# A GEGLU feed-forward kernel: bf16 products done ahead in nine groups of sixteen matmuls in place of eighteen groups of eight

## The chip, the core and the metric

The kernel runs on one core of a Trainium2 chip. The metric is the device time of one execution in microseconds (us). TensorE (PE) multiplies, its weight loads have a row of their own in the profile (PEld), VectorE (DVE), ScalarE (ACT) and GpSimd (POOL) do element-wise work, and SyncE (SP) issues nearly all the transfers. Every engine runs its own list of instructions in order and waits for others through semaphores.

## The reference

```
B, S, D, F = 32, 32, 1024, 3584
x: (B, S, D)   w_gate, w_up: (D, F)   w_down: (F, D)   all bf16

def reference(x, w_gate, w_up, w_down):
    return (_gelu(x @ w_gate) * (x @ w_up)) @ w_down
```

The gelu is the tanh approximation. There are N = 1024 rows of x; F = 3584 is cut into 28 blocks of 128, D = 1024 into 8 slices of 128.

## The kernel before

**Seven products in place of eight.** The kernel has two stages, and in each it treats a matrix product as a product of matrices of two by two blocks, done by Strassen's scheme in Winograd's form: seven block products instead of eight. In the first stage, for each of the 28 blocks `i` of F, four weight blocks (the two halves of D of the gate weights, a11 and a12, and of the up weights, a21 and a22) meet four blocks of x (two halves of D, two halves of N: B11, B12, B21, B22). Sums of weight blocks (S1 to S4) and of x blocks (T1 to T4) are kept as float32r, a 32-bit type that TensorE multiplies; the blocks themselves are bf16. Every product is four matmuls of 128x128 weights by 128x512 (function `product`, line 111).

Two of the seven products need no sums: the first, a11 by B11, and the second, a12 by B21, both bf16. The first is copied out of PSUM by ACT (L187, tile `e1`) to serve later as a seed of other products, and then the second is added onto the same bank of PSUM; its total is the gate's pre-activation for the first half of N, and ACT takes its gelu (L193, tile `gl0`). So for one block, the first product and ACT's copy come before the second product, and the second product comes before the gelu that gives the bank back. These two products depend on weights and x alone and are done ahead of the others: variable `done` counts the blocks whose first product has been issued.

The other five are float32r. In the trace they are told by their tiles: the sixth product is `x<-T,s`, the fourth `x<-T,c`, the fifth `y<-T,s`, the seventh `x<-T,s` again, the third `y<-B,s`, and the two bf16 products are `a<-xt,gw`. The sixth, seventh and fourth follow each other onto one bank `X[i]`, which ACT seeds with the copied first product (L199); ACT copies it out after the sixth (L214, tile `e2`) and after the seventh (L227, `e3`), and DVE multiplies it after the fourth (L218). The fifth and third share a bank `Y[i]`, from which DVE makes sums (L229, L234), the second of which goes through ACT's gelu (L236).

**Order of the work.** It is written out by hand (`tc.manual_schedule`): each engine executes its instructions in the order of the program, and only waits are inserted. A lead-in (lines 255 to 262) issues first and second products of eight blocks in the order first n, first n+1, second n, second n+1. Blocks 0 and 1 then go through the other five products, with two calls of `ahead`. From line 296 a loop runs over the blocks 2 to 28. One iteration `i` issues: the sums S1 and S3 of block i+1 on POOL (L166, L167), the sixth product of `i`, the seed of i+1, the fourth product of i-1, the sums S2 (DVE, L171) and S4 (POOL, L175) of i+1, the fifth product of `i`, possibly a bf16 group, the seventh product of `i`, and the third product of i-1. An iteration without a bf16 group has 20 matmuls and is called bare below. `ahead` does the first product of block `done` and the second product of block `done - 1`, eight matmuls; it is called in every iteration but those in `ALONE`, until all 28 blocks are done. Weights are fetched on SP's queue at the end of even iterations, five gate tiles of two blocks being held (L84, L91).

**Buffers.** The PSUM pool has four banks for tag `p` (the `X`) and four for tag `q`, which the `A` of the bf16 products and the `Y` share. A pool hands out the buffer that was given back longest ago in the order of the program, and the first writer of it waits for the last reader of the tile before. `E1` tiles hold two blocks each in a ring of four; a ring buffer is free once the seeds of its two blocks have been issued and done.

The second stage (lines 328 to 485) multiplies by w_down in the same manner, its operands as prepared by the first; TensorE goes from one stage to the next without a pause.

The lines that the change and the prediction touch:

Of the kernel before, what the change touches and what calls it, by code (L numbers as in the profile page):

```python
# [12 lines left out]
def kernel(  # L13
# [31 lines left out]
    FT = F // P  # L45
# [3 lines left out]
    assert N == 2 * NB and DT % 2 == 0 and D % DB == 0 and FT % 4 == 0  # L49
    NWARM = 18  # L50
    LEAD = 8
    ALONE = (4, 7, 10, 13, 16, 19)
    KF = FT // 2
    TT = NT // 2
    JF = KF // 2
# [25 lines left out]
    def load_gate(c, queue, lo=0, hi=DT):  # L81
        if c not in WG:
            WG[c] = gw.tile([P, DT, 2 * P], bf16, name="gw", tag="gw")
        queue.dma_start(  # L84
            out=WG[c][:, lo:hi, :], in_=wg_r[:, lo:hi, 2 * c * P : (2 * c + 2) * P]
        )

    def load_up(c, lo=0, hi=4):
        if c not in WU:
            WU[c] = uw.tile([P, DT, 4 * P], bf16, name="uw", tag="uw")  # L90
        nc.sync.dma_start(  # L91
            out=WU[c][:, :, lo * P : hi * P],
            in_=wu_r[:, :, (4 * c + lo) * P : (4 * c + hi) * P],
        )
# [4 lines left out]
    def a11(i):  # L99
        return block(WG, 2, i, 0)  # L100

    def a12(i):
        return block(WG, 2, i, 1)
# [7 lines left out]
    def product(ps, lhs, rhs, first=True):  # L111
        for k in range(KH):
            nc.tensor.matmul(  # L113
                ps,
                lhsT=lhs[:, k, :],
                rhs=rhs[:, k, :],
                start=(first and k == 0),
                stop=(k == KH - 1),
                skip_group_check=True,
            )  # L120
# [4 lines left out]
    def psum_q(name):  # L125
        return psum.tile([P, NB], fp32, name=name, tag="q")

    with tc.manual_schedule():
# [35 lines left out]
        def early_sums(i, engine=nc.gpsimd):  # L164
            S1[i], S3[i] = weight_tile("s1"), weight_tile("s3")
            engine.tensor_tensor(S1[i], a21(i), a22(i), ALU.add)  # L166
            engine.tensor_tensor(S3[i], a11(i), a21(i), ALU.subtract)  # L167

        def second_sum(i):
            S2[i] = weight_tile("s2")  # L170
            nc.vector.tensor_tensor(S2[i], S1[i], a11(i), ALU.subtract)  # L171

        def late_sums(i, engine=nc.gpsimd):
            S4[i], C22[i] = weight_tile("s4"), weight_tile("c22")
            engine.tensor_tensor(S4[i], a12(i), S2[i], ALU.subtract)  # L175

        def copy_a22(i):
            nc.scalar.activation(C22[i], a22(i), ACT.Copy)
# [3 lines left out]
        def first_product(i):  # L182
            A[i] = psum_q("a")
            product(A[i], a11(i), B11)
            if i % 2 == 0:
                E1[i // 2] = ring.tile([P, 2, NB], fp32, name="e1", tag="ring")
            nc.scalar.activation(E1[i // 2][:, i % 2, :], A[i], ACT.Copy)  # L187

        def second_product(i):
            product(A[i], a12(i), B21, first=False)  # L190
            if i % 2 == 0:
                GL[i // 2] = half.tile([P, 2, NB], bf16, name="gl0", tag="half")
            nc.scalar.activation(GL[i // 2][:, i % 2, :], A[i], ACT.Gelu_apprx_tanh)  # L193
# [3 lines left out]
        def seed(i):  # L197
            X[i] = psum_p("x")
            nc.scalar.activation(X[i], E1[i // 2][:, i % 2, :], ACT.Copy)  # L199

        done = 0

        def ahead():
            nonlocal done
            if done < FT:
                first_product(done)
            if done:
                second_product(done - 1)
            done += 1

        def sixth_product(i):
            product(X[i], S2[i], T["T2"], first=False)
            E2[i] = epool.tile([P, NB], fp32, name="e2", tag="e2")
            nc.scalar.activation(E2[i], X[i], ACT.Copy)  # L214

        def fourth_product(i):
            product(X[i], C22[i], T["T4"], first=False)
            nc.vector.tensor_tensor(gT[:, i, 0:NB], GL[i // 2][:, i % 2, :], X[i], ALU.mult)  # L218

        def fifth_product(i):  # L220
            Y[i] = psum_q("y")
            product(Y[i], S1[i], T["T1"])

        def seventh_product(i):
            product(X[i], S3[i], T["T3"], first=False)
            e3 = epool.tile([P, NB], fp32, name="e3", tag="e3")
            nc.scalar.activation(e3, X[i], ACT.Copy)  # L227
            U1[i] = epool.tile([P, NB], bf16, name="u1", tag="u1")
            nc.vector.tensor_tensor(U1[i], Y[i], e3, ALU.add)  # L229

        def third_product(i):
            product(Y[i], S4[i], T["B22"], first=False)
            h1 = epool.tile([P, NB], bf16, name="h1", tag="h1", bufs=1)
            nc.vector.tensor_tensor(h1, Y[i], E2.pop(i), ALU.add)  # L234
            G1[i] = epool.tile([P, NB], bf16, name="gl1", tag="gl1")
            nc.scalar.activation(G1[i], h1, ACT.Gelu_apprx_tanh)  # L236

        def finish(i):
            nc.vector.tensor_tensor(gT[:, i, NB:N], G1.pop(i), U1.pop(i), ALU.mult)
# [23 lines left out]
        done = LEAD  # L263
# [5 lines left out]
        for k in range(KH):  # L269
            for i in range(2):  # L270
# [7 lines left out]
                )  # L278
        ahead()
        sixth_product(0)  # L280
        sixth_product(1)
        seventh_product(0)
        seventh_product(1)
# [12 lines left out]
        for i in range(2, FT + 1):  # L296
            here, prev, more = i < FT, i - 1 if i > 2 else None, i + 1 < FT
            if more:
                early_sums(i + 1)
            if here:  # L300
                sixth_product(i)
                if more:
                    seed(i + 1)
            if prev:
                fourth_product(prev)
            if more:
                second_sum(i + 1)
                late_sums(i + 1)
            if prev:
                finish(i - 2)  # L310
            if here:
                fifth_product(i)
            if here and i not in ALONE and done <= FT:
                ahead()
            if here:
                seventh_product(i)
                if more:
                    copy_a22(i + 1)
            if prev:
                third_product(prev)  # L320
            if here and i % 2 == 0:
                if i // 2 + 5 < FT // 2:
                    load_gate(i // 2 + 5, nc.sync)
                if i % 4 == 0 and i // 4 + 1 < FT // 4:
                    load_up(i // 4 + 1)
# [190 lines left out]
```

## Time and profile before

| What | Value |
|---|---|
| Three runs | 277.67, 278.09 (median), 278.29 us |
| The profiled execution's own time | 277.56 us |
| Its span, first to last instruction | 275.8 us, so 1.76 us lie around it |
| Mean granted TensorE clock | 0.999 |
| TensorE busy | 270.0 us of the span (98%) |
| ACT, DVE, POOL busy | 138.1, 189.2, 88.6 us |
| The loop of lines 296 to 326, from the first sixth product to the second stage | 33.64 to 184.58 us |

How to read the rows: a row of a timeline gives the start, the duration, the engine, the line in the kernel, the operation, the tile written and the tiles read, the shapes and, in square brackets, the idle time of that engine before it and what ended it. Rows of one kind that follow each other are merged, with their number behind an x; some matmul records are missing from a trace, so that a group of eight may read x7. Matmuls are pipelined: one that lasts 379 or 389 ns in the records is followed by the next after 216 or 227 ns. Where the text speaks of nanoseconds from one start to the next, these are single records of the same trace. A window row gives busy time and number of instructions of each engine in a stretch of time.

### The profile page before, as it was taken

How to read it: one execution, taken by the hardware profiler on the slowest of the kernel's cores; microseconds unless marked ns; L12 is line 12 of the kernel's file. 1: busy time of each engine (PE TensorE's matmuls, PEld its weight loads, DVE VectorE, ACT ScalarE, POOL GpSimd, SP SyncE). 2: the span in 40 equal slices, each digit the busy share in tenths (PEclk: the TensorE clock that was granted, in tenths of full speed). 3: DMA queues.
4: the chain of work that ended last, by engine and by line, in shares of the span. 5: the costliest groups of instructions: out<-in, count | busy, mean ns of one | idle time of the engine just before them, and what ended most of it. 6: DMA issues, size and time to landing. Idle time of an engine off the chain costs nothing.

```text
span 275.8 us, 3328 instructions
## 1 busy us (share of the span) xinstructions
PE 270.0 (98%) x1179; PEld 190.5 (69%) x1194; DVE 189.2 (69%) x227; ACT 138.1 (50%) x237; POOL 88.6 (32%) x81
## 2 busy tenths in 40 slices
PE   8999999999999999999999999999999999999995
PEld 3446767777677776777766777764447888888883
DVE  0279865667666676666766555759994999999900
ACT  2488475665656665666656666532100082870311
POOL 0000484458554585545854444600000000000000
PEclk9999999999999999999999999999999999999999
DMA  8996420522062071152420120259702000000221
GB/s 194 286 280 157 150 71 5 156 77 76 18 212 76 0 225 37 46 154 76 154 76 9 67 58 22 88 188 324 239 0 76 2 0 0 0 2 0 96 96 38
DMA packets 40912, 26.42 MB, mean 96 GB/s; under 512 B 9152, under 2 KB 40896, under 8 KB 40896
## 3 DMA queue, kind: packets, MB, share of 16 engines
q1 hardware_dynamic: 40224, 25.82, 32.0%
q10 hardware_dynamic: 672, 0.39, 0.5%
q8 instruction: 9, 0.15, 0.2%
q14 instruction: 7, 0.06, 0.1%
HBM read 22.02 MB, written 2.10 MB: 87 GB/s over the span
## 4 chain that ended last, share of the span: by engine, by line
PE 96%; DMA 3%; issue 0%; ACT 0%
PE x L113 28%; PE x L371 18%; PE y L113 18%; PE a L113 17%; PE y L371 9%; PE z L371 4%; DMA xt<-in_x_dram 3%; PE y L271 1%; ACT o_sb L483 0%
## 5 line engine op out<-in xcount | busy, mean ns | idle before, releaser
L113 PE MATMUL x<-T,s 128*128 128x512 f32 x224 | 63.5, 408 | 0.0
L113 PE MATMUL a<-xt,gw 128*128 128x512 bf16 x212 | 51.0, 380 | 1.1 <-DMA xt<-in_x_dram 0.4
L175 POOL TENSOR_TENSOR s<-gw,s 128x512 fp32r<-128x512 bf16 x26 | 30.4, 1171 | 62.4 <-PE y L113 61.7
L113 PEld LDWEIGHTS x<-T,s 128*128 128x128 f32 x224 | 41.7, 188 | 10.8 <-ACT e L214 0.4
L229 DVE TENSOR_TENSOR u<-y,e 128x512 bf16<-128x512 f32 x28 | 19.2, 690 | 34.8 <-ACT e L227 34.1
L171 DVE TENSOR_TENSOR s<-s,gw 128x512 fp32r<-128x512 f32 x28 | 40.8, 1457 | 0.0
L113 PEld LDWEIGHTS <-gw 128*128 128x128 bf16 x224 | 20.2, 98 | 27.6 <-issue 5.7
L218 DVE TENSOR_TENSOR gT<-gl,x 128x512 bf16<-128x512 bf16 x28 | 19.1, 686 | 18.4 <-PE x L113 18.4
L236 ACT ACTIVATE gl<-h 128x512 bf16<-128x512 bf16 x28 | 17.7, 631 | 27.4 <-DVE h L234 27.4
L113 PE MATMUL x<-T,c 128*128 128x512 f32 x112 | 30.2, 393 | 0.0
L113 PE MATMUL y<-B,s 128*128 128x512 f32 x112 | 30.0, 391 | 0.0
L167 POOL TENSOR_TENSOR s<-gw,uw 128x512 fp32r<-128x512 bf16 x25 | 29.2, 1168 | 0.0
L166 POOL TENSOR_TENSOR s<-uw 128x512 fp32r<-128x512 bf16 x25 | 29.1, 1164 | 0.0
L187 ACT ACTIVATE e<-a 128x512 f32<-128x512 f32 x28 | 16.7, 597 | 22.9 <-PE a L113 22.8
L113 PE MATMUL y<-T,s 128*128 128x512 f32 x104 | 27.8, 389 | 0.0
L371 PE MATMUL x<-tc,sc 128*128 128x512 f32 x112 | 25.7, 389 | 0.0
L113 PEld LDWEIGHTS y<-B,s 128*128 128x128 f32 x112 | 21.0, 188 | 4.8
L113 PEld LDWEIGHTS x<-T,c 128*128 128x128 f32 x112 | 20.9, 188 | 4.8 <-ACT e L227 0.5
L371 PEld LDWEIGHTS x<-tc,sc 128*128 128x128 f32 x112 | 21.0, 188 | 4.4
L227 ACT ACTIVATE e<-x 128x512 f32<-128x512 f32 x28 | 16.8, 599 | 14.4 <-PE x L113 14.4
L113 PEld LDWEIGHTS y<-T,s 128*128 128x128 f32 x104 | 19.5, 188 | 4.1
L371 PEld LDWEIGHTS <-gT 128*128 128x128 bf16 x112 | 10.9, 98 | 13.2 <-issue 0.3
(52 smaller groups left out, 325.0 us busy)
## 6 DMA issues: line engine op xcount, KB each, us to landing
gw<-in_w_gate_dram SPq DMA_DIRECT2D x13, 512.0 KB, 3.9
uw<-in_w_up_dram SPq DMA_DIRECT2D x6, 1024.0 KB, 6.4
v<-in_w_down_dram SPq DMA_DIRECT2D x5, 512.0 KB, 3.8
v<-in_w_down_dram SPq DMA_DIRECT2D x4, 640.0 KB, 7.9
v<-in_w_down_dram SPq DMA_DIRECT2D x8, 256.0 KB, 4.3
out_dram<-o_sb SPq DMA_DIRECT2D x15, 128.0 KB, 1.7
uw<-in_w_up_dram SPq DMA_DIRECT2D x2, 512.0 KB, 6.0
gw<-in_w_gate_dram ACTq DMA_DIRECT2D x1, 256.0 KB, 4.4
```

The source lines that it names most:

```text
L113: nc.tensor.matmul(ps, lhsT=lhs[:, k, :], rhs=rhs[:, k, :], start=(first and k == 0), stop=(k == KH - 1), skip_group_check=True,)
L166: engine.tensor_tensor(S1[i], a21(i), a22(i), ALU.add)
L167: engine.tensor_tensor(S3[i], a11(i), a21(i), ALU.subtract)
L171: nc.vector.tensor_tensor(S2[i], S1[i], a11(i), ALU.subtract)
L175: engine.tensor_tensor(S4[i], a12(i), S2[i], ALU.subtract)
L187: nc.scalar.activation(E1[i // 2][:, i % 2, :], A[i], ACT.Copy)
L218: nc.vector.tensor_tensor(gT[:, i, 0:NB], GL[i // 2][:, i % 2, :], X[i], ALU.mult)
L227: nc.scalar.activation(e3, X[i], ACT.Copy)
L229: nc.vector.tensor_tensor(U1[i], Y[i], e3, ALU.add)
L236: nc.scalar.activation(G1[i], h1, ACT.Gelu_apprx_tanh)
L271: nc.tensor.matmul(Y[i], lhsT=S1[i][:, k, :], rhs=T["T1"][:, k, :], start=(k == 0), stop=(k == KH - 1), skip_group_check=True,)
L371: nc.tensor.matmul(ps, lhsT=lhs[:, i, t * P : (t + 1) * P], rhs=rhs[:, i, :], start=(first and j == 0 and i == 0), stop=(last and j == JF ...
```

## The change

The tuple `ALONE`, iterations that did without a bf16 group, gives way to `PAIRS`, iterations that have one. A new function `pair_ahead` does the work of two calls of `ahead` at once, in another order: the second product of block `done - 1`, the first product of `done`, the first product of `done + 1`, the second product of `done`. The last iteration of `PAIRS` (26) finds all first products done and only does the second product of block 27.

```
-    ALONE = (4, 7, 10, 13, 16, 19)
+    PAIRS = (2, 5, 8, 10, 13, 16, 18, 21, 24, 26)
...
+        def pair_ahead():
+            nonlocal done
+            second_product(done - 1)
+            if done < FT:
+                first_product(done)
+                first_product(done + 1)
+                second_product(done)
+            done += 2
...
-            if here and i not in ALONE and done <= FT:
-                ahead()
+            if i in PAIRS:
+                pair_ahead()
```

Before, groups stood in iterations 2, 3, 5, 6, 8, 9, 11, 12, 14, 15, 17, 18 and 20 to 25, with a group of four matmuls in 26. After, groups of sixteen stand in 2, 5, 8, 10, 13, 16, 18, 21 and 24, with the same group of four in 26.

## The prediction

> **What bounds the kernel now.** I read the page first: engine shares, the granted clock and the chain that ended last.
>
> ```profile
> span 275.8 us, 3328 instructions
> ...
> PE 270.0 (98%) x1179; PEld 190.5 (69%) x1194; DVE 189.2 (69%) x227; ACT 138.1 (50%) x237; POOL 88.6 (32%) x81
> ...
> PEclk9999999999999999999999999999999999999999
> ...
> PE 96%; DMA 3%; issue 0%; ACT 0%
> ```
>
> TensorE is the bound, at full clock in every slice. Work that moves on ACT, DVE, POOL or a queue costs nothing unless TensorE comes to wait for it; a wait of TensorE costs its full length. Then the loop of the change (lines 296 to 325) by windows, each from the start of one fifth product to the next:
>
> ```profile
> core 0: us, PE busy (x) PEld busy (x) DVE busy (x) ACT busy (x) POOL busy (x), PEclk, DMA share, GB/s
> 57.16:63.46 6.30, 6.30 (x30) 4.46 (x28) 3.81 (x5) 3.80 (x8) 3.41 (x4) 1.00 0.00 1
> 63.46:68.00 4.54, 4.54 (x21) 3.71 (x20) 3.82 (x5) 2.59 (x6) 3.41 (x4) 1.00 0.41 115
> ```
>
> The first is an iteration with a group of eight bf16 matmuls beside its 20 float32r ones, the second a bare one of 20. Next, the stage that already does what the change will do often: in the lead-in (timeline) a first product is followed by another first product and then by the second product on the first one's bank, which must wait for ACT's copy.
>
> ```profile
> 7.96 5.99 PE L113 MATMUL a<-xt,gw 128*128 128x512 bf16 x27 [0.43 <-DMA xt<-in_x_dram]
> ...
> 9.02 0.60 ACT L187 ACTIVATE e<-a 128x512 f32<-128x512 f32 x1 [5.66 <-PE a L113]
> 9.88 0.60 ACT L187 ACTIVATE e<-a 128x512 f32<-128x512 f32 x1 [0.27 <-PE a L113]
> ...
> 10.74 0.60 ACT L193 ACTIVATE gl<-a 128x512 bf16<-128x512 f32 x1 [0.27 <-PE a L113]
> ```
>
> 27 matmuls start within 5.99 - 0.38 = 5.61 us, 216 ns each: that wait cost nothing. In the loop (timeline again):
>
> ```profile
> 68.21 0.58 ACT L214 ACTIVATE e<-x 128x512 f32<-128x512 f32 x1
> ...
> 68.91 1.90 PE L113 MATMUL a<-xt,gw 128*128 128x512 bf16 x7
> 70.05 0.60 ACT L187 ACTIVATE e<-a 128x512 f32<-128x512 f32 x1 [0.77 <-PE a L113]
> ...
> 70.46 1.27 PE L113 MATMUL x<-T,s 128*128 128x512 f32 x4
> 70.85 0.60 ACT L193 ACTIVATE gl<-a 128x512 bf16<-128x512 f32 x1 [0.21 <-PE a L113]
> ```
>
> To be seen: the copy L214 of the sixth product ends at 68.79, 0.12 before TensorE goes on at 68.91. Two more places of the timeline show what late ACT work does. First, one of the few waits of TensorE; then iteration 2, where ACT is behind:
>
> ```profile
> 25.61 0.60 ACT L214 ACTIVATE e<-x 128x512 f32<-128x512 f32 x1 [0.20 <-PE x L113]
> ...
> 26.26 0.76 PEld L113 LDWEIGHTS x<-T,s 128*128 128x128 f32 x4 [0.20 <-ACT e L214]
> ```
>
> ```profile
> 35.46 1.90 PE L113 MATMUL a<-xt,gw 128*128 128x512 bf16 x8
> ...
> 36.58 0.59 ACT L199 ACTIVATE x<-e 128x512 f32<-128x512 f32 x1
> ...
> 37.21 0.60 ACT L187 ACTIVATE e<-a 128x512 f32<-128x512 f32 x1
> ...
> 37.70 0.59 ACT L193 ACTIVATE gl<-a 128x512 bf16<-128x512 f32 x1
> ```
>
> **The change part by part.** The count of matmuls, ACT, DVE and POOL instructions and DMAs stays. Eighteen groups of eight become nine of sixteen; the last group of four (second product of block 27, iteration 26) stays in its place. No DMA moves in its queue: gate loads are issued at the same lines and wait for POOL's sums, which the pairs do not touch. Blocks 22 and 23 move most, from iterations 20 and 21 to 18; their gate tile is asked for in iteration 12, six iterations ahead, with 3.9 us to landing.
>
> *Fewer switches.* A group adds 6.300 - 4.547 = 1.753 us to an iteration (mean of the windows above in ns), while eight bf16 matmuls at 215.8 take 1.726: 27 ns per group are the price of switching from float32r to bf16 and back. Nine go: -0.24 us. Its ends: 0, and -0.35 if the 39 ns by which an iteration with a group exceeds 20 x 226.7 + 8 x 215.8 all belong to the group.
>
> *The two new ACT waits of a pair.* Inside a pair the second product of the new block waits for the copy (L187) that began four matmuls before. Also the second first product needs a bank: banks go out in the order in which they were given back (this gives all 56 bank numbers of the program before), and by that order it takes, in eight of nine pairs, the bank that the gelu (L193) of the same pair's opening second product gave back, again four matmuls before. The chain is matmul 379, start of ACT 37 later, 597 of copy or gelu: 1,013 ns from the start of the last matmul. TensorE is due 5 x 215.8 = 1,079 after it. 66 ns are left, and in the lead-in the same 66 left no loss. Cost 0 for a wait of this form.
>
> Where the copy carries a second wait (for the ring buffer that its own earlier seed frees), ACT starts 97 after the matmul instead of 37 (52.90 and 70.05 in the loop: idle 0.83 and 0.77 before it, and only 0.21 before the gelu that follows). The chain is then 1,073. TensorE's weight load starts 52 after ACT's end (26.21 to 26.26), so a loss of 1,073 + 52 - 1,079 = 46 ns. I expect it for the pairs of iterations 5, 8 and 10, whose ring buffer was freed one or two iterations before; later pairs come three or more after. 3 x 46 = +0.14 us. Ends: 0, and 18 x 46 = 0.83.
>
> *Iteration 2.* ACT's order becomes gelu of 9, copy of 10, copy of 11, gelu of 10 behind a queue that runs to 37.18. Unwaited ACT work goes out every 0.49 there: gelu at 37.07, copy of 10 at 37.56 to 38.16, TensorE free at 38.21; due is 35.46 + 0.23 + 11 x 0.216 = 38.06. +0.15 us. This spares the 41 ns that the fourth product of iteration 3 now waits for ACT's copy (38.97). Net +0.11, ends -0.04 and +0.42 (each of the two starting only 0.03 after the other's end).
>
> *Two bare iterations in a row.* New is a bare iteration behind a bare one (4, 7, 12, 15, 20, 23). Behind a bare iteration the copy L214 ends 0.12 before the fifth product's end (68.79 against 68.91; 0.11 to 0.15 at 85.94, 103.09, 120.23, 137.41; 0.19 at 51.58), behind one with a group 0.25. Today a bf16 group stands there, which does not need the copy; now the seventh product does, as float32r, whose weight load itself waits. At 26.21 the copy also ended 0.12 before the matmul was due, and the next matmul came 268 instead of 227 later: 41 lost. Five of the six: +0.21 us; iteration 4 keeps 0.19. Ends: 0 and 6 x 0.1 = 0.6. What is late next: nothing adds up, because DVE's L218 and POOL's L175 start anew from TensorE's products in every bare iteration (DVE 3.82 and POOL 3.41 of 4.54 us busy).
>
> The sum: -0.24 + 0.14 + 0.11 + 0.21 = +0.22 us. Against the profiled execution (span 275.8, 1.76 around it, 277.56 in all) that is 277.78. It lies 0.53 below the median of the three runs, 278.09; carried to the median: 278.3.
>
> **The rivals.** *Even (0.68)*: the sum above, within 0.2% (0.56 us, about what a measurement can tell from no change). Own range 277.7 (terms at their low ends, -0.39) to 278.6.
>
> *Slower by the close waits (0.20)*: every pair's two ACT waits miss. Place: the matmuls opening the second first product and the second product; price 18 x 46 instead of 3 x 46, so 278.3 + 0.69 = 279.0. It decides once the chain is over 1,027 (1,079 - 52), only 14 ns beyond what the rows show, and loses 18 ns in all for each ns more. For it: the gelu's 599 and the copy's 601 at their longest. Against it: lag 37 and 597 in every undisturbed group of the loop.
>
> *Slower by the bank (0.03)*: the bank freed last is handed out at once, so the first new product stands behind the gelu: 1,013 + 52 - 216 = 0.85 us, nine times 7.6, less 0.24: 285.5. Against it are the 56 bank numbers. The Trainium skill (Perfetto Trace Analysis, Optimizing Tensor Performance, Matmuls) speaks against the change in this sense: independent groups should rotate through different banks so that ACT's emptying of one overlaps the next group. By that rule a bank reused within a pair would cost time; by the lead-in's rows four matmuls already hide the emptying.
>
> *The clock (0.01)*: if TensorE fell to the rate of its first warm matmuls (427 ns each) in the pairs, 9 x 16 x 0.211 = 30 us, 308. The clock row shows full speed throughout, with idle spots of 0.4. The Trainium skill (TensorE: Matmul & The Clock Gate, A second HAM failure mode: psum-queue depth-cycling) reports such an oscillation where TensorE idles briefly between groups that cycle through banks; no row here shows it.
>
> *Faster (0.08)*: switches cost more than the windows show. From 33.64 to 184.58 the loop takes 150.94; 520 x 226.7 + 148 x 215.8 make 149.8. If all 1.12 beyond came from the eighteen groups, half would go and no wait be added: 277.5.
>
> **How the numbers follow.** Likeliest: 278.3. Faster 0.08, same 0.68, slower 0.20 + 0.03 + 0.01 = 0.24. The range reaches from the faster case, 277.5, to just over the close waits, 279.1; outside lie the bank, the clock and the tails of both.
>
> **What would show it.** Right: nine bf16 groups of 16 at 216 ns per start, sixteen matmuls and no idle time inside; a pair's iteration 8.03 us, bare ones 4.55 and the second of two 4.59; weight loads waiting for ACT L214 in five or six places; a short gap in the pair of iteration 2. Wrong: waits of `a` for L193 or L187 in all pairs (close waits); gaps of 0.85 before a first product (bank); a second bare iteration much over 4.6, so that DVE or POOL do fall behind; a clock digit below 9.

## The result, and the profile after

The changed kernel takes 278.88 us (median; 278.60 to 279.09), the kernel before 277.68 in the same comparison (277.62 to 278.29). The ratio is 1.0042, 95% interval 1.0032 to 1.0052: slower by 1.2 us. That lies inside the range on record (277.5 to 279.1), but it is not the likeliest case, "even" at 278.3. The kernel came out slower, and not for the reason that the forecast gave for that case.

The profiled execution has a span of 277.3 us. TensorE is still the bound and still at full clock (page of the changed kernel):

```profile
span 277.3 us, 3330 instructions
...
PE 271.0 (98%) x1180; PEld 190.8 (69%) x1194; DVE 189.2 (68%) x227; ACT 138.0 (50%) x237; POOL 88.8 (32%) x81
...
PEclk9999999999999999999999999999999999999999
```

Windows from one fifth product to the next, iterations 6, 7, 11, 12 and 13. Of two bare iterations in a row the second is the slower one (7 and 12, against 6 and 11), and the iteration with the group of sixteen, 13, is as cheap as forecast:

```profile
core 0: us, PE busy (x) PEld busy (x) DVE busy (x) ACT busy (x) POOL busy (x), PEclk, DMA share, GB/s
59.36:63.91 4.55, 4.55 (x21) 3.76 (x20) 3.82 (x5) 2.13 (x5) 3.42 (x4) 1.00 0.01 2
63.91:68.99 5.08, 4.82 (x21) 3.68 (x20) 3.80 (x5) 3.19 (x6) 3.41 (x4) 1.00 0.35 103
89.73:94.28 4.55, 4.55 (x21) 3.72 (x20) 3.81 (x5) 2.60 (x6) 3.41 (x4) 1.00 0.39 115
94.28:98.93 4.65, 4.65 (x22) 3.68 (x20) 3.82 (x5) 2.81 (x6) 3.42 (x4) 1.00 0.00 2
98.93:106.95 8.02, 7.95 (x36) 5.25 (x36) 3.82 (x5) 5.14 (x10) 3.41 (x4) 1.00 0.63 196
```

Inside that pair (timeline) ACT's gelu and its copies follow each other at the 0.27 us of idle time that the lead-in showed, and the matmuls on record start 215 to 217 ns apart:

```profile
100.06 3.40 PE L113 MATMUL a<-xt,gw 128*128 128x512 bf16 x15
100.91 0.60 ACT L193 ACTIVATE gl<-a 128x512 bf16<-128x512 f32 x1 [0.80 <-PE a L113]
...
101.78 0.60 ACT L187 ACTIVATE e<-a 128x512 f32<-128x512 f32 x1 [0.27 <-PE a L113]
102.64 0.60 ACT L187 ACTIVATE e<-a 128x512 f32<-128x512 f32 x1 [0.27 <-PE a L113]
```

Where the 1.2 us went can be read off the lengths of the iterations, single records in ns. From the fifth product of iteration 2 to the second stage, the loop takes 150.03 us before and 151.22 after; the second stage, 91.19 and 91.21, does not change.

| Place | Difference to before, us |
|---|---|
| Nine times a pair and a bare iteration, 8.0265 + 4.547, in place of 2 x 6.300 | -0.24 |
| Pairs of iterations 5, 8, 10: 8.093 in place of 8.027 | +0.20 |
| Iterations 2 and 3: 11.886 in place of 11.753, beside the switch saved there | +0.16 |
| Second bare iterations 12, 15, 20, 23: 4.647, 4.633, 4.679, 4.687 in place of 4.547 | +0.46 |
| Second bare iteration 7: 5.081 in place of 4.547 | +0.53 |
| Other iterations, up to 33 ns each, and the end of the loop | +0.08 |

Nearly half of the loss is the one iteration 7. In the second bare iteration 12 (timeline) ACT's copy L223 (L214 before the change) ends at 95.06, and the weight load of the seventh product starts at 95.17 instead of 94.96, where the matmul ahead of it starts:

```profile
93.94 0.63 ACT L245 ACTIVATE gl<-h 128x512 bf16<-128x512 bf16 x1 [1.00 <-DVE h L243]
...
94.48 0.58 ACT L223 ACTIVATE e<-x 128x512 f32<-128x512 f32 x1
...
95.17 0.77 PEld L113 LDWEIGHTS x<-T,s 128*128 128x128 f32 x4 [0.25 <-POOL s L166]
95.21 1.16 PE L113 MATMUL x<-T,s 128*128 128x512 f32 x4
```

The waits name POOL here. The weight load stands behind two waits, POOL's and ACT's, so who really held it is a question for an experiment.

### The profile page after: what moved, and what is told of

It is laid out like the page before. It is cut to its first block, busy times and chain, and to the rows that moved or that the text cites. A ratio compares the mean times of both kernels' runs of the same rounds, so it can differ in the third digit from the quotient of the medians.

```text
span 277.3 us, 3330 instructions
## 1 busy us (share of the span) xinstructions
PE 271.0 (98%) x1180; PEld 190.8 (69%) x1194; DVE 189.2 (68%) x227; ACT 138.0 (50%) x237; POOL 88.8 (32%) x81
## 4 chain that ended last, share of the span: by engine, by line
PE 94%; DMA 3%; ACT 1%; issue 1%; DVE 0%; ACTq 0%
PE x L113 27%; PE x L380 18%; PE a L113 17%; PE y L113 17%; PE y L380 9%; PE z L380 4%; DMA xt<-in_x_dram 3%; PE y L280 1%; DVE u L238 0%; DVE h L243 0%; ACT e L236 0%; ACT o_sb L492 0%; ACT e L223 0%; ACT c L178 0%; ACT gl L245 0%
## 5 line engine op out<-in xcount | busy, mean ns | idle before, releaser
L113 PE MATMUL x<-T,s 128*128 128x512 f32 x224 | 62.3, 403 | 0.3 <-ACT e L223 0.3
L113 PE MATMUL a<-xt,gw 128*128 128x512 bf16 x213 | 48.6, 379 | 1.3 <-DMA xt<-in_x_dram 0.6
L238 DVE TENSOR_TENSOR u<-y,e 128x512 bf16<-128x512 f32 x28 | 19.3, 691 | 37.1 <-ACT e L236 35.3
L113 PEld LDWEIGHTS <-gw 128*128 128x128 bf16 x224 | 20.9, 98 | 27.8 <-issue 4.1
L245 ACT ACTIVATE gl<-h 128x512 bf16<-128x512 bf16 x28 | 17.7, 631 | 28.9 <-DVE h L243 28.9
L167 POOL TENSOR_TENSOR s<-gw,uw 128x512 fp32r<-128x512 bf16 x25 | 29.3, 1173 | 0.7 <-PE x L113 0.7
L166 POOL TENSOR_TENSOR s<-uw 128x512 fp32r<-128x512 bf16 x25 | 29.1, 1165 | 0.0
L236 ACT ACTIVATE e<-x 128x512 f32<-128x512 f32 x28 | 16.8, 599 | 20.7 <-PE x L113 20.7
L193 ACT ACTIVATE gl<-a 128x512 bf16<-128x512 f32 x28 | 16.7, 596 | 10.6 <-PE a L113 10.3
```

The costliest lines, as they stand in the source:

```text
L113: nc.tensor.matmul(ps, lhsT=lhs[:, k, :], rhs=rhs[:, k, :], start=(first and k == 0), stop=(k == KH - 1), skip_group_check=True,)
```

## The experiments

Theory: TensorE waits for ACT's copy of the sixth product wherever a bare iteration follows a bare one, and that is due to where the groups stand; the order inside the pair costs little. Rivals: the pair's own waits; POOL, as the waits say; chance, for iteration 7.

### The changed kernel again, and bare iterations two in a row without pairs

> The changed kernel once more. Theory (the new order makes TensorE wait for ACT's copy L223 in a bare iteration that follows a bare one): iterations 12, 15, 20 and 23 again take 4.63 to 4.69 us in place of 4.55, the pairs of iterations 5, 8 and 10 again show one matmul 260 ns after the one before. Open: iteration 7, which took 5.08 us. If it belongs to the order it takes 5.08 again; if DVE's late sum L238 (0.4 us after everything that it needs) was chance, it takes 4.65.

It took 278.68 us, in one run. Iterations 12, 15, 20 and 23 took 4.634, 4.626, 4.627 and 4.633, the pairs of 5, 8 and 10 8.086 to 8.087, and iteration 7 5.074. DVE's sum L238 of iteration 6 again came 0.51 us after DVE's work before it, where 0.10 would do, so 0.4 us late. So the loss of iteration 7 was not chance; it belongs to the program.

```
-    ALONE = (4, 7, 10, 13, 16, 19)
+    ALONE = (6, 7, 12, 13, 18, 19)
```

> Groups of eight as before, no pairs, but the six bare iterations stand two in a row (6 and 7, 12 and 13, 18 and 19). Theory: bare iterations 7, 13 and 19 lose about 0.09 us each to ACT's copy though there is no pair, 0.3 us in all, 0.1% slower than before. Rival (the order inside the pair and its new waits cost the time): these iterations take 4.55 us like the first of each two and the time is that of before.

278.39 us, ratio 1.0025 (1.0015 to 1.0035): slower than expected, without a single pair. Windows of iterations 12 and 13:

```profile
core 0: us, PE busy (x) PEld busy (x) DVE busy (x) ACT busy (x) POOL busy (x), PEclk, DMA share, GB/s
93.78:98.35 4.57, 4.57 (x21) 3.71 (x20) 3.81 (x5) 2.62 (x6) 3.41 (x4) 1.00 0.01 2
98.35:102.98 4.63, 4.63 (x21) 3.68 (x20) 3.83 (x5) 2.76 (x6) 3.44 (x4) 1.00 0.82 255
```

Iterations 13 and 19 took 4.626, iteration 7 took 5.026, and every iteration with a group of eight 6.300 (but the third, 6.323). So bare iterations two in a row cost 0.7 us by their place alone, with groups of eight and no pair. The expected 0.3 us was too little because iteration 7 lost 0.48 here too.

### ACT's copy ahead of the gelu

In the kernels so far ACT's list has the gelu of the third product (L245) ahead of the copy of the next sixth product, and the gelu waits for DVE. The edit puts it behind; the new function `late_gelu` does the gelu of the tile that waits in `H1`:

```
         def third_product(i):
...
-            nc.scalar.activation(G1[i], h1, ACT.Gelu_apprx_tanh)
+            H1[i] = h1
...
                 sixth_product(i)
+                late_gelu()
                 if more:
                     seed(i + 1)
```

> The changed kernel with one more edit: ACT takes the gelu of the third product (L245) after the copy of the next sixth product and not ahead of it, so that this copy ends about 0.5 us earlier. Theory (that copy is what TensorE waits for): the second bare iterations take 4.55 us, 0.4 us less in all, or 0.9 us less if iteration 7 has the same cause; 278.5 or 278.0 us against 278.9. Rival (POOL, which the waits name, is late with its sums): they still take 4.63 to 4.69 us, and the time stays at 278.9.

277.78 us, ratio to the kernel before 1.0003 (0.9994 to 1.0012), 1.1 us less than the changed kernel's 278.88. Windows of iterations 7 and 12, and a timeline of iteration 12:

```profile
63.73:68.30 4.57, 4.57 (x21) 3.68 (x20) 3.80 (x5) 3.07 (x6) 3.40 (x4) 1.00 0.40 115
93.61:98.16 4.55, 4.55 (x21) 3.75 (x20) 3.81 (x5) 2.74 (x6) 3.41 (x4) 1.00 0.01 2
```

```profile
93.30 0.60 ACT L223 ACTIVATE e<-x 128x512 f32<-128x512 f32 x1 [1.05 <-DVE h L243]
...
93.79 0.62 ACT L253 ACTIVATE gl<-h 128x512 bf16<-128x512 bf16 x1
...
94.27 1.17 POOL L167 TENSOR_TENSOR s<-gw,uw 128x512 fp32r<-128x512 bf16 x1
94.29 0.87 PEld L113 LDWEIGHTS x<-T,s 128*128 128x128 f32 x4
```

The copy ends at 93.90, 0.62 before the matmul at 94.52 that needs it, and the weight load goes on without a pause. POOL works at the same point of the iteration as before. TensorE's waits put down to POOL fall from 1.6 us in five places (first line, the changed kernel) to 0.2 in one (second line, this kernel):

```profile
PEld x L113 <- POOL s L166: 1.6, 5, 0.7
```

```profile
PEld x L113 <- POOL s L166: 0.2, 1, 0.2
```

So the copy was what held TensorE; the name in the waits was wrong. The kernel says so too: the seventh product reads the sum S3 (L167), which POOL made an iteration earlier, and the sum named, S1 (L166), is for a later product.

> The kernel before with the same later gelu and nothing else. Theory: before, no float32r product stood right behind a late copy, so nothing is gained: within 0.1 us of the kernel before. Rival (the later gelu is worth something by itself, wherever it stands): 0.4 us or more faster than before.

The same edit on the kernel before: 277.52 us, ratio 0.9993 (0.9984 to 1.0002). That is 0.16 us less in the medians, a little more than the 0.1 expected, but the interval includes no difference at all, and the loop of the profiled run is 0.05 us shorter. So of the 1.1 us that the edit is worth in the changed kernel most is a loss that the change had brought.

### The half microsecond of iteration 7

Timeline of DVE in the changed kernel, iterations 6 and 7:

```profile
60.16 1.59 DVE L171 TENSOR_TENSOR s<-s,gw 128x512 fp32r<-128x512 f32 x1
61.68 0.41 DVE L248 TENSOR_TENSOR gT<-gl,u 128x512 bf16<-128x512 bf16 x1
62.60 0.69 DVE L238 TENSOR_TENSOR u<-y,e 128x512 bf16<-128x512 f32 x1 [0.51 <-ACT c L178]
63.20 0.68 DVE L243 TENSOR_TENSOR h<-y,e 128x512 bf16<-128x512 f32 x1
```

From there the delay goes on to ACT and to TensorE's weight load, in the same trace:

```profile
61.43 0.60 ACT L236 ACTIVATE e<-x 128x512 f32<-128x512 f32 x1 [1.06 <-PE x L113]
...
63.98 0.63 ACT L245 ACTIVATE gl<-h 128x512 bf16<-128x512 bf16 x1 [1.43 <-DVE h L243]
...
64.52 0.58 ACT L223 ACTIVATE e<-x 128x512 f32<-128x512 f32 x1
...
65.21 0.76 PEld L113 LDWEIGHTS x<-T,s 128*128 128x128 f32 x4 [0.65 <-POOL s L166]
```

The sum L238 needs ACT's copy L236, which had ended at 62.03, and follows DVE's own work that ended at 62.09; it started at 62.60. In every kernel up to here it is the 64th recorded instruction of DVE, semaphore instructions counted. In the kernel before, DVE was idle at that place for 1.73 us for another reason.

```
+        spare = gpool.tile([P, 8], bf16, name="spare")
+        for _ in range(6):
+            nc.vector.memset(spare, 0.0)
         warm = [psum_p("warm") for _ in range(4)]
```

> The changed kernel with six tiny memsets more on DVE in the lead-in, where DVE is idle; they write a tile that nothing reads. In every kernel so far DVE pauses 0.47 us between the 63rd and 64th of its recorded instructions, which in the changed kernel is the sum L238 of iteration 6. Theory (the pause is tied to the place in DVE's list): it moves six instructions ahead, into idle time of the pair of iteration 5, and iteration 7 takes 4.65 us instead of 5.08; 0.4 us less in all. Rival (it belongs to that sum or to that time): iteration 7 takes 5.08 us again.

278.36 us, ratio 1.0026 (1.0014 to 1.0037), some 0.5 us less than the changed kernel. Iteration 7 took 4.686. DVE at the same point now:

```profile
61.38 0.41 DVE L251 TENSOR_TENSOR gT<-gl,u 128x512 bf16<-128x512 bf16 x1
61.90 0.69 DVE L241 TENSOR_TENSOR u<-y,e 128x512 bf16<-128x512 f32 x1
```

The pause of 0.4 us is gone from this sum, whose data come at the same point of the iteration as ever. The 64th instruction is now the sum of iteration 5, for which DVE waits 3.5 us anyway. Nor is the pause tied to a moment of the execution: in later_pairs and best, below, DVE takes the same 0.47 us ahead of its 64th instruction at 58.5 and 58.3 us, over 3.5 us earlier than here. So it is tied to the place in DVE's list. It made the sum late, with it the gelu, with it the copy behind the gelu, and with that TensorE: four steps, in a place with almost no slack.

### The early pairs

```
-    PAIRS = (2, 5, 8, 10, 13, 16, 18, 21, 24, 26)
+    PAIRS = (2, 7, 9, 11, 13, 16, 18, 21, 24, 26)
```

> The changed kernel with the pairs of iterations 5, 8 and 10 moved to 7, 9 and 11, so that the ring buffer of a copy was given back three iterations before. Theory: no copy L187 in these pairs has a second wait, no matmul in them starts 260 ns after the one before, and they take 8.03 us instead of 8.09. Rival (the 65 ns come of the pair itself, as its two waits on ACT miss): they take 8.09 us in their new places.

278.11 us in one run. The pairs of 7, 9 and 11 took 8.027 each, the bare iterations 15, 20 and 23 still 4.674, 4.687 and 4.634; the pair in iteration 2 lost what it had lost before (7.341 + 4.545). Iterations 3 to 6 are now bare, four in a row, and 5 and 6 lost 0.09 and 0.05. Window of iteration 7:

```profile
60.34:68.36 8.02, 7.95 (x36) 5.23 (x36) 3.81 (x5) 5.56 (x10) 3.40 (x4) 1.00 0.22 65
```

In the changed kernel the three early pairs each had one matmul 260 or 261 ns behind the one before, in place of 216; in the new places ACT starts the copy 37 ns after the matmul instead of 97, and that gap is gone. The pair's own waits cost nothing there.

### The price of a switch

```
-            if here and i not in ALONE and done <= FT:
-                ahead()
+            group = here and i not in ALONE and done <= FT
+            if group and done < FT:
+                first_product(done)
             if here:
                 seventh_product(i)
...
+            if group:
+                second_product(done - 1)
+                done += 1
```

> The kernel before with every group of eight cut in two groups of four: the first product ahead of the seventh product, the second product behind it. Twice the switches, no pair, no new bare iteration. Theory (a group costs 27 ns for the switch from float32r to bf16 and back): an iteration with a group takes 6.327 us in place of 6.300, 18 x 0.027 = 0.5 us more in all, 0.17%. Rival (a switch costs nothing and the gain of the pairs was something else): 6.300 us and the time of before.

278.50 us, ratio 1.0031 (1.0019 to 1.0043). Iterations with a cut group take 6.325 to 6.328 us, as worked out (but the third, 6.336). Window of iteration 6:

```profile
57.75:64.08 6.33, 6.33 (x30) 4.38 (x28) 3.90 (x5) 3.75 (x8) 3.40 (x4) 1.00 0.01 4
```

The loop is 0.91 us longer than before, not 0.5: iteration 2 with its part of the next took 0.49 more, where ACT is behind and one weight load waited 0.7 us for its copy L214. The price per switch is the 26 to 27 ns of the undisturbed iterations.

### All edits together

Later gelu, groups of eight in iterations 2 and 3, pairs in 7, 9, 11, 13, 16, 18, 21 and 24:

> The changed kernel with three edits: the later gelu, groups of eight in iterations 2 and 3 in place of the first pair, and the other early pairs moved to 7, 9 and 11. Theory: all four losses are gone and the switches saved remain, eight of them, 0.2 us: 277.4 us against 277.7 of the kernel before, 0.1% faster; pairs take 8.027 us and bare iterations 4.53 to 4.56. Rival (something in the pairs goes on costing): 277.7 us or more.

277.40 us, ratio to the kernel before 0.9990 (0.9981 to 0.9999): a gain of 0.3 us that the runs only just tell from none. Windows of iterations 7 and 8:

```profile
60.05:68.08 8.03, 7.96 (x37) 5.25 (x36) 3.82 (x5) 5.55 (x10) 3.42 (x4) 1.00 0.23 65
68.08:72.63 4.55, 4.55 (x21) 3.76 (x20) 3.81 (x5) 2.60 (x6) 3.43 (x4) 1.00 0.00 0
```

The loop takes 149.83 us, 0.19 less than before the change; eight switches saved at 27 ns make 0.22. Against the kernel before with the later gelu alone (277.52) the difference is too small for these runs.

## Why the prediction was right or wrong

The sum of the prediction was a loss of 0.22 us; measured were 1.20. That the time still lies inside the range is luck. The forecast stood on the 278.09 of three runs, and the same kernel took 277.68 in the comparison, which hides 0.41 of the miss; carried to 277.68, the range would have ended at 278.7, below the measured 278.88. Its upper end was set for the close waits, too, which did not come. One of the signs named for being wrong did come: a second bare iteration much over 4.6 us (iteration 7, 5.08), with DVE late.

**Fewer switches, -0.24 us:** right. Pairs took 8.026 to 8.027 where no copy was late, bare iterations 4.545 to 4.547 at their shortest, and cutting the groups in two cost 26 to 27 ns per group.

**The two ACT waits of a pair, 0:** right. The margin of 66 ns read off the lead-in held wherever ACT was not late, with the bank that the gelu had just given back too: in the five pairs from iteration 13 on, and in all pairs of later_pairs but that of iteration 2, no bf16 matmul on record in these two traces started more than 217 ns after the one before it. The rival of the close waits (0.20) fell, though its 279.0 lies nearest to the measured time; so did the bank and the clock (granted clock 1.00 in every window).

**The copy with two waits, +0.14:** right in place and cause (iterations 5, 8, 10; ACT starting 96 to 97 ns after the matmul; a gap of 260 or 261 ns), a little small in size: 66 ns a pair instead of 46, as the float32r matmuls behind the group came some 20 ns later still; why was not tested.

**Iteration 2, +0.11 net:** the pair's loss was 165 ns in one gap, against 150 forecast. The wait of the fourth product in iteration 3, which I had counted as spared, stayed (267 ns between two matmuls as before): 0.16 in place of 0.11.

**Two bare iterations in a row, +0.21:** here the prediction failed, in the size. Place and cause were right: the copy of the sixth product, seen by gelu_later and bare_rows. But four iterations lost 0.09 to 0.14 instead of 0.04, and iteration 7 lost 0.53. The 41 ns came from a row in which the weight load had one wait. The weight load of the seventh product has two, for POOL's sum and for ACT's copy, and the wait for ACT is an instruction of its own ahead of the load (51 ns in the records of the changed kernel, from 95.10 to 95.15). So the load started 114 ns after the copy's end in place of 52, and the second matmul came 305 to 311 ns after the first in place of 227. The trace of before shows these 114 ns in the bare iteration 13, where the copy ends at 98.41:

```profile
97.83 0.58 ACT L214 ACTIVATE e<-x 128x512 f32<-128x512 f32 x1
...
98.52 0.79 PEld L113 LDWEIGHTS x<-T,s 128*128 128x128 f32 x4
```

That was the row to take the price from. Nor do the records of before bear out that TensorE has no wait for the copy where a bf16 group follows: the same 51 ns instruction stands ahead of the groups (at 68.83, 38 ns after the copy's end). But there the group's first matmul still came on time, 230 ns after the one before it, with a late copy as with an early one. And "nothing adds up" overlooked that the chain from DVE's sum over the gelu to the copy had some 0.1 us of slack, so that 0.4 us by which DVE's sum was late went on to TensorE (iteration 7 took 5.08 with the pause and 4.69 without); DVE's pause could be seen in the trace of before only as a part of an idle time of 1.73 us.

With 0.99 in place of 0.21 for this term, and the 0.05 and 0.06 of the two before it, the sum of +0.22 becomes about +1.1; the loop measured +1.19.

## What to carry to other kernels

When a bound engine's filler work is gathered into fewer, larger groups, price the places that the filler leaves as well as the groups: where the filler could start in spite of a helper's late answer, there may now stand an instruction that loses time to it. At each such place take the time between the end of the helper's work and the moment when the bound engine needs it, and subtract the bound engine's reaction time, read off a row whose instruction has as many waits. Count a chain with 0.1 us of slack as a risk, since a pause of a helper engine can pass through it, as it did here in iteration 7. Where the order of a helper's list decides, moving one waiting instruction behind one that the bound engine needs can be worth more than the regrouping itself: here 1.1 us against 0.2.

## What the runs showed of the hardware that was not expected

DVE pauses at a fixed place of its list: between its 63rd and 64th recorded instruction it took 0.47 us from the start of a 21 ns semaphore instruction to the start of the sum behind it, in the changed kernel, its repetition, bare_rows, gelu_later, later_pairs and best (idle time before the sum 507 to 510 ns), and six more instructions ahead of it moved the pause off that sum (idle 103 ns). What it is was not settled. The profile lists a DMA packet of kind "instruction" at 63.28, after the pause of the changed kernel. In all ten traces such a packet starts when 63 to 65 of DVE's recorded instructions have started (at 59.65 in later_pairs, at 56.71 in shifted), so it goes with the same place in the list; that the one causes the other was not shown.

A wait of TensorE for several engines was put down to POOL although ACT's copy decided it (1.6 us in five places): the profile names one releaser of several.
